# Attention and gated feed-forward on one core: merged steps and new pacing in the second pass, spread vector work elsewhere

## The chip, the cores and the metric

The kernel runs on one core of a Trainium2 chip. The metric is the device time of one execution in microseconds, given as the median of several runs. The core's engines are TensorE (PE in the profile), VectorE (DVE), ScalarE (ACT), GpSimd (POOL) and SyncE (SP, here only the issuer of DMAs). Each executes its own instructions in the order in which the program emits them; semaphores tie the engines together.

## The reference, cut to what matters

Four sequences of 448 tokens with 12 heads of 64 go through causal attention. The result, 1792 rows of 768, is normalised by its root mean square and goes through a gated feed-forward layer with 1536 hidden columns, all in float32.

```python
scores = np.matmul(q, k.transpose(0, 1, 3, 2)) / np.sqrt(64)
scores = np.where(mask, -1e9, scores)            # causal
attn = exp(scores - max) / (sum + 1e-9)
x = np.matmul(attn, v) -> reshaped to (1792, 768)
xn = x / np.sqrt(np.mean(x * x, -1) + 1e-6) * rms_g
g = xn @ w_gate
out = (g * sigmoid(g) * (xn @ w_val)) @ w_out
```

## The kernel before

**Blocks of tokens.** Rows are cut into three blocks: the first 256 queries of two sequences (512 columns), the same of the other two (512), and the rest of all four (768). Attention is cut into 60 units, each with two heads: 12 of kind 0 for block 0, 12 of kind 0 for block 1, and 36 for block 2. Of these 36, each group of six has four of kind 1 (128 queries, 384 keys) and two of kind 2 (64 queries and 448 keys, two sequences at once).

**The steps of a unit.** *Scores* (`steps_s`, L171): matmuls into PSUM (L191), on DVE mask and row minimum (L200), then exp on ACT, a reciprocal on DVE and the division on POOL or ACT, the latter three posted some slots later. *Transposes* (`steps_t`, L233), one step for each head `e`: three or four transposes into a PSUM bank (L248), then one copy to SBUF tile `pt` (L252 on DVE, L254 on ACT). In the second pass all of them use the one bank `t`, so the next step's transposes must wait for the copy. *Products* (`steps_a`, L258): matmuls of `v` and `pt` into bank `a` (L274) and a copy out (L289).

**Slots.** A stretch ahead does the attention of block 0. Then two passes do the feed-forward of block 0 and of block 1, each over 36 weight tiles `s`; one tile is three *slots* (`k0` in 0, 2, 4), and a slot issues six matmuls of 512 columns (L435 to L437, high and low parts of float32 split into two). After its six matmuls a slot may run attention steps: pass 0 those of block 1, pass 1 those of block 2. `AT` (L54) says over how many of the pass's 108 slots the steps are spread, by L851: `while done < goal and (done - at) < (goal - at) * i / AT[w_]`. `tick()` ends a slot, and `post(d, fn)` delays work by `d` slots.

**Steps of the second pass.** `round_of_two` (L750) takes two units p and p+1 in five steps: a *visit* (scores of p+3 and p+4, products of p and p+1), and the transposes of p+2 and of p+3, two steps each. 18 rounds and two steps ahead of them come to 90 steps in pass 1, the last four of them empty, over 77 slots. So 13 slots hold two steps. Two steps, the transposes of unit 25, stand at the end of pass 0; there 37 steps are spread over 101 slots.

**The end of pass 1.** When all steps are done (L871) `x_steps` (L483) scales block 2 (L514), makes the sums of a seven-product scheme for 2x2 blocks (L523) and splits the operands into high and low parts `ch` and `cl` (L473, and L475 on DVE or L102 on POOL), one entry of its list a slot. Besides, DVE makes the low parts `w_l` of every second weight tile (L391) and evicts results `ob` (L443), whose stores to DRAM (L445) stand in SP's one queue with the weight loads. `quad_load` (L560) loads the first weights for block 2 and `quad_prep` (L569) splits them; the fourth one (L564) is posted eight slots after the top of tile 69.

**Block 2 and the end.** Block 2's gate and value products run through `quad_product` and `quad_result` (L582, L596): seven products of nine matmuls for each of 12 weight tiles. Then 21 products of 18 matmuls (L695) make the output. Ahead of them `h_sums` (L674) makes two sums and a difference from the hidden tile for each of three parts, all in the first three products; the difference (L679) is read first by operand 12, which is split beside product 8.

**Root mean square.** `rms` (L330) has one matmul with ones, a square root on ACT and four reciprocals of 128 columns on DVE (L338), one behind the other.

Of the kernel before, what the change touches and what calls it, by code (L numbers as in the profile page):

```python
# [39 lines left out]
ENDS = [max(i for i, u in enumerate(UNITS) if u[0] == g) + 1 for g in range(NG)]  # L40
# [10 lines left out]
WR = 4  # L51
WARM = [9, 0, 0, 2]
EXTRA = 4
AT = [101, 77]  # L54
XT = 768
HX = XT // 2
RING = 6
# [4 lines left out]
def attention_ffn(ctx: ExitStack, tc: tile.TileContext, qk0, qk1, qk2, v, v2, w, g, out, out2):  # L62
# [7 lines left out]
    nc = tc.nc  # L70
# [59 lines left out]
    def post(delay, fn):  # L130
        if delay <= 0:
            fn()
        else:
            later.setdefault(now[0] + delay, []).append(fn)
# [98 lines left out]
    def steps_t(p):  # L233

        if not 0 <= p < len(UNITS):
            return []
        _, kind, _, _, _, _ = UNITS[p]
        pr = hs[p]
        kb = KB[kind]

        def some(e):
            pt = pr["pt", e] = pt_p.tile([P, W], F32, tag=f"pt{e}", name="pt")
            ps = bank("x" if e and p < ENDS[1] + 1 else "t")
            at = 0
            for j in range(NKB[kind]):
                for o, wd in blocks(kind):
                    if kb * j < wd:
                        nc.tensor.transpose(ps[:kb, at: at + P],  # L248
                                            pr["sp"][e][:, o + kb * j: o + kb * (j + 1)], ident)
                        at += P  # L250
            if kind or (e and p < ENDS[0]):
                nc.vector.tensor_copy(pt[:kb, :at], ps[:kb, :at])  # L252
            else:
                nc.scalar.copy(pt[:kb, :at], ps[:kb, :at])  # L254

        return [lambda e=e: some(e) for e in (0, 1)]
# [73 lines left out]
    def rms(b, sq):  # L330

        ps = bank("t")
        nc.tensor.matmul(ps, ones, sq, start=True, stop=True)
        r = rinv[b] = rm_p.tile([P, W], F32, tag="rms", name="rms", bufs=2)
        nc.scalar.activation(r, ps, AF.Sqrt, bias=eps, scale=1.0 / DM)
        for i in range(W // P):
            sl = slice(i * P, (i + 1) * P)
            nc.vector.reciprocal(r[:, sl], r[:, sl])  # L338


    w64 = w.bitcast(I32).rearrange("u p (c t) -> u p c t", t=2)
# [218 lines left out]
    def quad_load(v, n):  # L560
        f, g_ = divmod(v, 2)
        t = wr_p.tile([P, DM], F32, tag="w", name="w_q")
        if n == 3:
            nc.sync.dma_start(out=t[:, : HX], in_=w32[2 * (f + 6) + g_][:, HX:])  # L564
        else:
            nc.sync.dma_start(out=t, in_=(w32[2 * f + g_], wy[v], wz[v])[n])
        wt["q", v, n] = t
# [103 lines left out]
    def h_part(p):  # L671
        return [hid[:, 6 * k: 6 * k + 6, HX * e + P * p: HX * e + P * (p + 1)] for e in (0, 1) for k in (0, 1)]

    def h_sums(p):  # L674
        a11, _, a21, a22 = h_part(p)
        s1, s2 = f2["s", p] = [side["s"].tile([P, 6, P], F32, tag=n, name=n, bufs=3) for n in ("s1", "s2")]
        nc.vector.tensor_tensor(s1, a21, a22, op=ALU.add)  # L677
        nc.vector.tensor_tensor(s2, s1, a11, op=ALU.subtract)  # L678
        nc.vector.tensor_tensor(a21, a11, a21, op=ALU.subtract)  # L679

    def h_operand(q):
# [68 lines left out]
    def round_of_two(p):  # L750


        def visit():
            for q in (p, p + 1):
                post(2, lambda q=q: load_v(q + 2))
            for f in steps_s(p + DP) + steps_s(p + DP + 1):
                f()
            fs = steps_a(p), steps_a(p + 1)
            for i in (0, 1):
                for f in fs:  # L760
                    f[i]()

        return [visit] + [lambda q=q, i=i: (steps_t(q) or 2 * [lambda: None])[i]()
                          for q in (p + 2, p + 3) for i in (0, 1)]


    def warm(n):
# [4 lines left out]
    with tc.manual_schedule():  # L772
# [9 lines left out]
        for p in range(-DP, ENDS[1]):  # L782
            steps += round_steps(p)
            if p + 1 in ENDS:
                ends.append(len(steps))
        steps += [lambda i=i: steps_t(ENDS[1] + 1)[i]() for i in (0, 1)]
        for p in range(ENDS[1], len(UNITS), 2):
            steps += round_of_two(p)
            if p + 2 in ENDS:
                ends.append(len(steps))  # L790
        done = 0
        n_pre = ends[0] + EXTRA
# [11 lines left out]
        n = 0  # L804
# [25 lines left out]
        for s in range(2 * NU):  # L830
            w_ = s // NU
            if s == NU:
                assert len(xh) == 12
                xrs.close()
                side["wrx"] = pool("wrx", 4, ffn1, side="left", reuse_waits="tile")
            if s % NU == 0:
                at, goal = done, ends[w_ + 1] + 2 * (w_ == 0)
            if s + 7 < NU:
                post(T["ld"], lambda s=s: load_w(s + 7))
            n = s + 6 - 2 * NU  # L840
            if n >= 0:
                if n < 4:
                    post(8, lambda n=n: quad_load(0, n))
            elif s + 6 >= NU:
                post(T["ld2" if NU <= s + 6 < NU + 2 * NF else "ld1"], lambda s=s: load_w(s + 6))
            for k0 in (0, 2, 4):
                ks = [k for k in (k0, k0 + 1) if (s, k) not in early]
                if ks:
                    ffn_part(s, ks)
                i = 3 * (s % NU) + k0 // 2 + 1  # L850
                while done < goal and (done - at) < (goal - at) * i / AT[w_]:  # L851
                    steps[done]()
                    done += 1
                if i >= 73 and w_ == 0:
                    split_x()
                if k0 == 0:
                    convert(s + 5)
                if k0 == (0 if s < 3 else 4):
                    split_w(s + 3)
                for fn in prep.pop(now[0], []):  # L860
                    fn()
                if todo:
                    for fn in todo.pop(0):
                        fn()
                n = 3 * (s - 2 * NU + 2) + k0 // 2
                if n in (0, 3, 5):
                    quad_prep(0, (0, 3, 5).index(n))
                if n in (2, 4):
                    quad_load(1, n // 2 - 1)
                tick()  # L870
                if todo is None and done == len(steps) and i >= AT[1] + 1:  # L871
                    assert s % NU >= 2 * NF
                    ffn1.close()
                    att.close()
                    side["xc"] = pool("xc", 1, tail, side="right", reuse_waits="tile")
                    side["sm"] = pool("sm", 1, tail, side="right", reuse_waits="tile")
                    todo = x_steps()
# [49 lines left out]
        for q in range(21):  # L927
            i, p = divmod(q, 3)
            ps_ = out_product(i, p)
            if i:  # L930
                wo_split(3 * (i + 1) + p)
                wo_load(3 * (i + 2) + p)
            out_result(i, p, ps_)
            if not i:
                h_sums(p)
            h_operand(q + 4)


# [46 lines left out]
```

## Time and profile before

| what | value |
|---|---|
| median of 3 runs | 727.82 us (725.52 to 728.54) |
| the profiled execution's own time | 726.79 us |
| its span in the trace | 724.6 us |
| PE busy | 675.3 us, 93% of the span |
| DVE, ACT, POOL busy | 535.8, 370.9, 361.8 us |
| mean granted clock of TensorE | 0.995 |

The span runs from the first to the last instruction of the profiled execution; what lies around it is 2.2 us. PE is busy for most of it, so time can come only from the 49 us in which PE idles, and from stretches in which its clock is granted at less than full speed.

### The profile page before, as it was taken

The page shows a single profiled execution, that of the slowest core. Times are in us where ns is not written, and L with a number is a line of the kernel's source. Part 1 is how long each engine was busy: PE and PEld are TensorE (multiplying, and loading weights), DVE is VectorE, ACT ScalarE, POOL GpSimd, SP SyncE. Part 2 cuts the span into 40 slices and gives each one's busy share as a digit, 9 for nine tenths or more (in the row PEclk, how much of TensorE's full clock was granted, in tenths as well). Part 3 has the DMA queues.
Part 4 walks back from the last instruction along what each step waited for, and adds up shares of the span by engine and source line. Part 5 has one row for each costly group of instructions (what it writes and reads, how often), then busy time and mean ns, then how long its engine had stood idle before and what let it go on. Part 6 is the DMA issues. An engine that isn't in the chain of part 4 may idle for free. (4 is left out here: it accounts for less than half of the span.)

```text
span 724.6 us, 11938 instructions
## 1 busy us (share of the span) xinstructions
PE 675.3 (93%) x4106; PEld 547.4 (76%) x4106; DVE 535.8 (74%) x1029; ACT 370.9 (51%) x832; POOL 361.8 (50%) x313
## 2 busy tenths in 40 slices
PE   9778889999999899989999998999899999999898
PEld 6455567677776666667767676787799999999887
DVE  4976899799998456767676767369386768689773
ACT  6958777777765234346253534335333433355341
POOL 4987445455556334646655565664354536402120
PEclk9999999999999999999999999999999999999999
DMA  7746477867776538575657555422557576452541
GB/s 255 254 146 204 153 261 254 276 223 252 270 237 245 182 113 248 159 249 164 228 169 261 170 181 171 146 99 98 182 176 247 183 250 232 156 154 77 153 119 65
DMA packets 71355, 138.80 MB, mean 192 GB/s; under 512 B 7744, under 2 KB 39232, under 8 KB 71296
## 3 DMA queue, kind: packets, MB, share of 16 engines
q1 hardware_dynamic: 71296, 138.05, 58.1%
q8 instruction: 32, 0.52, 0.3%
q14 instruction: 27, 0.22, 0.1%
HBM read 104.21 MB, written 33.82 MB: 190 GB/s over the span
## 5 line engine op out<-in xcount | busy, mean ns | idle before, releaser
L208 POOL TENSOR_SCALAR sp<-sp,rs 128x384 f32<-128x384 f32 (+3 forms) x132 | 87.1, 677 | 107.3 <-DVE rs L212 106.3
L435 PE MATMUL m_ps<-xh,w_h 128*128 128x512 f32 x282 | 120.2, 426 | 2.5 <-DVE t_sb L459 2.5
L437 PE MATMUL m_ps<-xh,w_l 128*128 128x512 f32 x282 | 111.1, 394 | 1.7 <-POOL w_l L102 1.7
L436 PE MATMUL m_ps<-xl,w_h 128*128 128x512 f32 x282 | 110.5, 392 | 0.0
L203 ACT ACTIVATE sp<-sp,nm 128x384 f32<-128x384 f32 (+3 forms) x168 | 87.2, 522 | 45.6 <-DVE nm L200 45.6
L102 POOL TENSOR_TENSOR a_l<-w_q,a_h 128x768 fp32r<-128x768 f32 x24 | 47.9, 1994 | 69.8 <-ACT a_h L473 69.6
L274 PEld LDWEIGHTS a_ps<-pt,v_r 128*64 128x64 f32 (+1 forms) x864 | 40.4, 137 | 37.6 <-issue 15.1
L274 PE MATMUL a_ps<-pt,v_r 128*64 128x128 f32 (+2 forms) x864 | 57.5, 267 | 10.4 <-DVE pt L252 6.7
L252 DVE COPY pt<-t_ps 128x384 f32<-128x384 f32 (+1 forms) x71 | 42.6, 599 | 32.9 <-PE t_ps L248 32.8
L248 PE MATMUL t_ps<-ident,sp 128*128 128x128 f32 (+1 forms) x309 | 51.4, 278 | 16.6 <-DVE pt L252 11.9
L435 PEld LDWEIGHTS m_ps<-xh,w_h 128*128 128x128 f32 x282 | 53.1, 188 | 14.8 <-issue 4.9
L102 POOL TENSOR_TENSOR w_l<-w_r,w_h 128x768 fp32r<-128x768 f32 x30 | 60.1, 2006 | 8.2 <-ACT w_h L389 8.2
L437 PEld LDWEIGHTS m_ps<-xh,w_l 128*128 128x128 f32 x282 | 52.9, 188 | 14.1 <-POOL w_l L102 2.1
L200 DVE CUSTOM_DVE_ANT_0 sp<-s_ps,mask 128x128 f32<-128x128 f32 (+3 forms) x136 | 49.8, 415 | 18.3 <-PE s_ps L191 16.8
L248 PEld LDWEIGHTS t_ps<-ident,sp 128*128 128x128 f32 (+1 forms) x309 | 36.7, 138 | 34.0 <-POOL sp L208 11.4
L375 POOL TENSOR_SCALAR w<-w 128x768 f32<-128x768 f32 x36 | 43.0, 1193 | 37.1 <-ACT w_c L374 27.9
L436 PEld LDWEIGHTS m_ps<-xl,w_h 128*128 128x128 f32 x282 | 53.3, 189 | 7.5
L435 PE MATMUL m_ps<-hh,w_h 128*128 128x512 f32 x144 | 58.9, 409 | 0.0
L437 PE MATMUL m_ps<-hh,w_l 128*128 128x512 f32 x144 | 57.1, 397 | 1.1 <-POOL w_l L102 0.9
L436 PE MATMUL m_ps<-hl,w_h 128*128 128x512 f32 x144 | 56.8, 394 | 0.0
L102 POOL TENSOR_TENSOR w_l<-w_c,w_h 128x768 fp32r<-128x768 f32 x18 | 38.8, 2157 | 30.0 <-ACT w_h L389 30.0
L377 DVE SCALAR_TENSOR_TENSOR w<-w 128x768 int32<-128x768 int32 x36 | 44.8, 1244 | 10.5 <-POOL w L375 10.4
(176 smaller groups left out, 1704.3 us busy)
## 6 DMA issues: line engine op xcount, KB each, us to landing
w<-in_w SPq DMA_DIRECT2D x36, 768.0 KB, 4.9
w<-w_c SPq DMA_DIRECT2D x36, 384.0 KB, 2.7
w_r<-w SPq DMA_DIRECT2D x36, 384.0 KB, 4.2
qk_r<-in_qk SPq DMA_DIRECT2D x48, 256.0 KB, 4.0
qk_r<-in_qk SPq DMA_DIRECT2D x12, 512.0 KB, 6.0
v_r<-in_v SPq DMA_DIRECT2D x12, 448.0 KB, 4.2
v_r<-in_v SPq DMA_DIRECT2D x24, 192.0 KB, 3.1
wy<-w_r SPq DMA_DIRECT2D x24, 192.0 KB, 5.2
```

Source lines behind the costliest of these rows:

```text
L102: nc.gpsimd.tensor_tensor(out_, a, b, op=op)
L200: nc.vector.tensor_tensor_reduce(out=sp, in0=ps, in1=mk, scale=nsc, scalar=3.0e38, op0=ALU.add, op1=ALU.min, accum_out=nm)
L203: post(T["exp" if p >= ENDS[0] else "exp0"], lambda: nc.scalar.activation(sp, sp, AF.Exp, bias=nm, scale=-1.0, accum_out=sm))
L208: pr["norms"].append(lambda: nc.gpsimd.tensor_scalar(sp, sp, rs, 1.0, op0=ALU.mult, op1=ALU.mult))
L248: nc.tensor.transpose(ps[:kb, at: at + P], pr["sp"][e][:, o + kb * j: o + kb * (j + 1)], ident)
L252: nc.vector.tensor_copy(pt[:kb, :at], ps[:kb, :at])
L274: nc.tensor.matmul(av_ps[e * D: (e + 1) * D, p % 2, q0: q0 + n], raw_v[p][:kb, h, j, e, :], pr["pt", e][:kb, a0: a0 + n], start=(j == 0), ...
L375: (T["c1"], lambda: nc.gpsimd.tensor_scalar(hf_, hf_, 0.0, 1.0, op0=ALU.mult, op1=ALU.mult)),
L377: (T["c2" if s >= 5 else "c20"], lambda: nc.vector.scalar_tensor_tensor(out=lo, in0=lo, scalar=29, in1=hi, op0=ALU.logical_shift_right, op ...
L435: nc.tensor.matmul(ps, wh[:, k, :], mh, start=(first and k == ks[0]), stop=False)
L436: nc.tensor.matmul(ps, wh[:, k, :], ml, start=False, stop=False)
L437: nc.tensor.matmul(ps, wl[:, k, :], mh, start=False, stop=(last and k == 5))
```

## The change

- `AT` goes from [101, 77] to [108, 73]: the steps of pass 0 are spread over all 108 slots, those of pass 1 over 73.
- `round_of_two` has four steps a round instead of five. The second transposes of unit p+1 move out of the round before into the first step, ahead of the scores and products, on PE and on DVE.
- The second transposes of unit 25 go from pass 0 into pass 1. The three steps behind the last visit, which would be empty, are deleted. Pass 0 now has 36 steps in 108 slots (one in every third slot), pass 1 has 69 in 73 slots (never two in one). The last visit comes in slot 72 instead of 73, and `x_steps` begins in slot 75 instead of 79.
- For block 1 the four reciprocals of `rms` are posted one a slot.
- The fourth weight load of block 2 is posted four slots after the top of tile 69 instead of eight, so it stands ahead of the third one, and of the store of the result of slot 102, in SP's queue.
- The difference in `h_sums` becomes `h_difference`, called beside products 6 to 8 instead of 0 to 2.

```diff
-AT = [101, 77]
+AT = [108, 73]
...
         for i in range(W // P):
             sl = slice(i * P, (i + 1) * P)
-            nc.vector.reciprocal(r[:, sl], r[:, sl])
+            post(i if b else 0, lambda sl=sl: nc.vector.reciprocal(r[:, sl], r[:, sl]))
...
         nc.vector.tensor_tensor(s2, s1, a11, op=ALU.subtract)
+
+    def h_difference(p):
+        a11, _, a21, _ = h_part(p)
         nc.vector.tensor_tensor(a21, a11, a21, op=ALU.subtract)
...
-        return [visit] + [lambda q=q, i=i: (steps_t(q) or 2 * [lambda: None])[i]()
-                          for q in (p + 2, p + 3) for i in (0, 1)]
+        def transposes(q, i):
+            fs = steps_t(q)
+            if fs:
+                fs[i]()
+
+        def last():
+            transposes(p + 1, 1)
+            visit()
+
+        return [last] + [lambda q=q, i=i: transposes(q, i) for q, i in ((p + 2, 0), (p + 2, 1), (p + 3, 0))]
...
-        steps += [lambda i=i: steps_t(ENDS[1] + 1)[i]() for i in (0, 1)]
+        steps.append(lambda: steps_t(ENDS[1] + 1)[0]())
         for p in range(ENDS[1], len(UNITS), 2):
             steps += round_of_two(p)
             if p + 2 in ENDS:
+                del steps[-3:]
                 ends.append(len(steps))
...
-                at, goal = done, ends[w_ + 1] + 2 * (w_ == 0)
+                at, goal = done, ends[w_ + 1] + (w_ == 0)
...
-                    post(8, lambda n=n: quad_load(0, n))
+                    post(8 if n < 3 else 4, lambda n=n: quad_load(0, n))
...
-            if not i:
+            if i == 0:
                 h_sums(p)
+            elif i == 2:
+                h_difference(p)
             h_operand(q + 4)
```

## Rows read from the trace of the kernel before

**Rows 1.** Busy time of each engine in the two passes (stretch, length, engines, granted clock).

```profile
71.45:256.42 184.97, 173.86 (x848) 131.55 (x847) 159.89 (x237) 123.19 (x263) 95.02 (x62) 0.99 0.67 231
256.42:464.28 207.86, 195.54 (x1543) 143.24 (x1542) 142.41 (x356) 90.80 (x227) 118.62 (x111) 1.00 0.60 192
```

**Rows 2.** PE's waits in 256.42 to 464.28 us: total, times, longest.

```profile
PE t_ps L248 <- DVE pt L252: 8.9, 8, 1.8
PE t_ps L248 <- POOL sp L208: 3.3, 4, 1.2
```

**Rows 3.** Single slots of pass 1, or ten bare ones, by stretch; columns as in Rows 1.

```profile
483.35:496.95 13.60, 13.60 (x62) 11.26 (x60) 12.06 (x20) 6.31 (x13) 7.73 (x8) 1.00 0.31 107
286.37:288.08 1.71, 1.71 (x12) 1.40 (x11) 0.69 (x3) 1.07 (x2) 0.70 (x2) 1.00 0.87 288
288.08:291.34 3.26, 2.25 (x16) 1.73 (x14) 2.29 (x4) 0.62 (x1) 3.26 (x4) 1.00 0.55 191
291.34:296.12 4.78, 4.78 (x45) 2.82 (x43) 2.69 (x9) 1.52 (x6) 3.42 (x3) 1.00 0.02 4
336.96:342.07 5.11, 5.11 (x48) 3.22 (x46) 4.54 (x12) 2.58 (x6) 3.21 (x3) 1.00 0.41 142
418.64:424.15 5.51, 5.51 (x86) 4.15 (x83) 4.45 (x12) 2.44 (x7) 4.36 (x4) 1.00 0.25 91
```

**Rows 4.** Timeline inside the last of these slots (start, duration, engine, line).

```profile
420.92 0.68 DVE L252 COPY pt<-t_ps 112x512 f32<-112x512 f32 x1
...
422.13 2.08 PE L274 MATMUL a_ps<-pt,v_r 112*64 112x64 f32 x64
```

**Rows 5.** The end of pass 0: one stretch of three slots, then DVE and PE in it.

```profile
237.69:246.87 9.18, 6.25 (x22) 4.79 (x21) 5.72 (x8) 1.56 (x2) 4.35 (x2) 0.81 0.56 195
...
235.84 3.37 DVE L338 RECIPROCAL rms<-rms 128x128 f32<-128x128 f32 x4
...
242.14 0.71 PE L248 MATMUL t_ps<-ident,sp 128*128 128x128 f32 x3 [2.93 <-DVE pt L252]
```

**Rows 6.** The last slots of pass 1: busy time, L514 alone, then DVE and PE.

```profile
476.74:505.19 28.45, 28.22 (x124) 22.87 (x123) 26.91 (x41) 13.81 (x27) 16.45 (x12) 1.00 0.36 119
...
477.34:481.55 4.21, 4.21 (x8) 1.00 0.71 249
...
476.74 0.69 DVE L443 SCALAR_TENSOR_TENSOR ob<-m_ps,rms 128x512 f32<-128x512 f32 x1 [6.19 <-PE m_ps L437]
...
495.97 1.77 DVE L391 TENSOR_TENSOR w_l<-w_r,w_h 128x768 fp32r<-128x768 f32 x1
...
497.79 0.50 PE L437 MATMUL m_ps<-hh,w_l 128*128 128x512 f32 x1 [0.23 <-DVE w_l L391]
```

**Rows 7.** The start of block 2's products: timeline of ACT, DVE and PE.

```profile
513.69 0.51 ACT L473 CAST a_h<-w_q 128x384 fp32r<-128x384 f32 x1 [6.30 <-DMA w_q<-w]
...
518.30 0.55 DVE L606 TENSOR_TENSOR u<-m,s_ps 128x384 f32<-128x384 f32 x1 [3.50 <-DMA out_t<-ob]
...
514.64 0.44 PE L578 MATMUL m_ps<-ch,a_h 128*128 128x384 f32 x1 [1.35 <-ACT m L601]
...
522.96 0.44 PE L578 MATMUL y_ps<-ch,a_h 128*128 128x384 f32 x1 [1.81 <-DVE c L612]
```

**Rows 8.** The output products: products 3 and 4, product 6, product 7; then DVE and PE.

```profile
657.72:663.96 6.24, 6.24 (x37) 6.24 (x37) 6.21 (x7) 4.01 (x6) 2.00 (x1) 1.00 0.11 37
667.08:674.28 7.20, 4.72 (x19) 3.77 (x19) 6.26 (x6) 2.16 (x5) 2.21 (x1) 0.87 0.61 185
674.28:678.14 3.86, 3.86 (x19) 3.86 (x19) 2.39 (x3) 1.54 (x2) 0.00 (x0) 0.79 0.62 170
...
656.82 0.95 DVE L679 TENSOR_TENSOR hid<-hid 128x768 f32<-128x768 f32 x1
...
669.01 2.59 DVE L475 TENSOR_TENSOR ol<-s,oh 128x768 fp32r<-128x768 f32 x1
...
672.52 0.69 PE L578 MATMUL s_ps<-a_l,oh 128*128 128x384 f32 x1 [2.06 <-DVE a_l L475]
```

## The prediction

> **What bounds the kernel now.** I read the busy time by stage first. PE is busy 195.5 of 207.9 us in the attention part of pass 1 and 173.9 of 185.0 us in pass 0, and no other engine comes near that in pass 1 (DVE 142.4); in pass 0 DVE is next with 159.9 [rows 1]. So PE's queue sets the time, and an edit gains only what it takes from PE's idle time or from a stretch at a lower clock. Next I read who PE waits for in pass 1: transposes, and nothing else. Eight waits are for the copy that empties bank t (8.9 us), four for the division on POOL (3.3 us) [rows 2]. Then I cut pass 1 into slots at the first matmul of each, and compared slots of the same content. At last I read the places outside this stretch with a PE gap over 1 us that the change touches: the end of pass 0 [rows 5], the start of block 2 [rows 7], output product 6 [rows 8]. Two gaps of over 2 us do more than idle: behind them the mean granted clock of the stretch is 0.81 and 0.79, that is, PE runs for a while at the lower of its two levels, 1.2 GHz [rows 5, 8].
>
> **Part 1, four steps a round in pass 1.** A bare slot costs 13.60 / 10 = 1.36 us, a slot with one transposes step 1.71, so it costs 0.35; two transposes steps in one slot should cost 2.06, but the slot shown took 3.26, 1.20 more, of which PE idles 3.26 - 2.25 = 1.01 [rows 3]. Eight such slots make the 8.9 us of waits. The four waits on POOL come where only two slots lie between a visit and the transposes that need its softmax; with three slots there is none. In the new order pass 1 has 69 steps in 73 slots. No slot has two steps, so no transposes stand straight behind others, and the first transposes of unit p+3 come at least three slots behind their scores. Both kinds of wait lose their cause: 8.9 + 3.3 = 12.2 us, and by the slot shown each of the 12 costs another 1.20 - 1.01 = 0.19 in refilling PE, 2.3 together: 14.5 us. The matmuls themselves stay the same in number.
>
> What is added is that each of the rounds has its transposes of p+1 right ahead of the scores, so products of p+1 wait for a copy that was issued in the same slot. The trace of before has this very slot twice, by the accident of its pacing. One took 5.11 us, where a visit of the same kind alone took 4.78 and the step adds 0.35: 5.13 expected, so the merger was free. The other, with the wider units, took 5.51, all of it PE busy [rows 3]. There the copy ran from 420.92 to 421.60, and the products began at 422.13, behind four pairs of score matmuls [rows 4]. The scores are the cover, about half a microsecond over what was needed, and the products of p come ahead of those of p+1 besides. If that cover is gone, each of the 17 mergers costs up to 1.20, the price of the uncovered slot, 20 us in all; the other bound is 0. I take 2.0, nearer to the two slots that show it free, for those rounds in which DVE is late. DVE's own work stays the same while the stretch shortens: 142.4 / (207.9 - 12.5) is 73% instead of 69%, no bound. **Gain 12.5 (14.5 less 2.0).**
>
> **Part 2, the end of pass 0.** Three slots there took 9.18 us where three bare ones and one step make 3 x 1.36 + 0.35 = 4.43 [rows 3, 5]. The excess of 4.75 has one cause: the four reciprocals hold DVE for 3.37 us, the copy out of bank t stands behind them, the next transposes wait 2.93 us, and the clock falls [rows 5]. In the new order the two steps of unit 25 are three slots apart (106 and the first of pass 1) and the reciprocals come one a slot, at the end of slots 103 to 106, where weight conversion, which filled DVE, is over. They are first read by the eviction behind slot 3 of pass 1, five slots later, so the delay costs nothing. The first waits for the square root on ACT; behind it on DVE are only a copy and evictions that come later. **Gain 4.5**, with bounds 3 (a gap of about 1 us stays) and 4.75. The rest of pass 0 only gets its steps further apart, 9 slots a round instead of 8.2. I give it nothing: DVE's 86% there [rows 1] eases a little, but every step now falls in the slot behind an eviction.
>
> **Part 3, the last 36 slots.** `x_steps` begins four slots sooner against the matmuls. On DVE this moves a long chain ahead of a deadline. Before, DVE was busy 26.9 of the 28.45 us from the eviction at 476.74 to 505.19: 12 scalings, 12 sums, 12 low parts, two `w_l` and two evictions. The `w_l` that slot 100 needs stood only behind three of the low parts, ended at 497.74, and still held PE for 0.23 us [rows 6]. Now it stands behind all twelve. Six scalings are done before that first `ob`, so ahead of it there remain 28.45 less 3.2 (six scalings at 4.21 / 8), 1.8 (the `w_l` itself), 0.7 (an eviction) and 1.4 (most of its idle 1.54): 21.4 us, start 498.1 in the times of before, end 499.1 with 0.95 for itself or 499.9 with 1.77. Against 497.74 that is 1.4 to 2.2 us more. The low parts can also be quicker, since POOL then has less beside them; bounds 0 and 2.6. **Loss 1.4.** The columns step now comes three slots (4.1 us) behind the last visit instead of six; I take no new wait for it.
>
> **Part 4, the start of block 2.** ACT waited 6.30 us for the fourth weights; the copy of the first product stands behind that split, and PE waited 1.35 for it. DVE then waited 3.50 for the store of the last result, which stood in SP's queue behind the same weights' buffer; this became PE's 1.81 us [rows 7]. SP's queue was late altogether because the store of slot 96 waited for its eviction at the end of the long chain. Now that eviction comes right behind the `w_l` of slot 100, and the fourth load is issued two places sooner: it has some seven slots (9 us) to land. The buffer that it takes moves the others by one place; the last load now waits for the third weights' split instead, on POOL, done about when the last slot ends, so the last store behind it need not cost DVE its 3.50. **Gain 3.0 of 1.35 + 1.81**; bounds 0 and 4.
>
> **Part 5, the sums.** Products 3 and 4 took 3.12 us each. Products 6 and 7 took 7.20 + 3.86, 4.82 over that [rows 8]: PE waited for `a_l` behind three differences of 0.95, then ran on at the low clock. Without them DVE comes to the low parts 2.8 us sooner, and the operand split that took 2.59 instead of 0.95, beside a POOL split, then falls ahead of that [rows 8]. Product 6 would find all three `a_l`. The differences now lie beside products 6 to 8. There DVE has about 3.1 us of work a product (a low part, an eviction, an operand, a difference) against PE's 3.12: full, so I leave 0.8 for a new wait. **Gain 4.0**, bounds 1.5 and 4.8.
> The Trainium skill, page "SBUF — State Buffer", section "SBUF: two separate sides", says that a VectorE operation with two SBUF inputs and a GpSimd operation shut each other out for a whole instruction, and speaks so against this move. The 2.59 us row agrees; each difference that meets a POOL split would take about 1.6 more by it, and one of them beside product 6 would leave 2.4 of these 4.0.
>
> **Sum.** 12.5 + 4.5 - 1.4 + 3.0 + 4.0 = 22.6 us from the profiled execution's own 726.79: 704.2. That execution lies 1.0 below the median of the runs (727.82), so I forecast 705.2.
>
> **Rivals.**
> *The chain on DVE takes the place of the old waits.* If the low parts meet POOL throughout, `w_l` ends 2.6 later than before and PE idles over 2 us; the clock then falls as behind product 6, where 4.82 were lost for 2.48 of idling (7.20 - 4.72) [rows 8]; I add 1.5. The stores then also come late and Part 4 gives nothing: 705.2 + (4.1 - 1.4) + 3.0 = 710.9. For it: DVE's chain has no free time. Against it: 1.77 for a `w_l` is already one beside POOL [rows 6], and 0.23 of waiting was all that it cost.
> *Pass 0 suffers from its even pacing.* If the steps, all behind evictions now, wait about 1.0 in each of eleven rounds, as PE's 1.01 in the slot with two steps [rows 3]: 716. Against it: a step in most slots of before cost nothing.
> *The merger isn't covered.* Most of the 17 wait for the copy, and the gain of pass 1 is lost, the waits having only moved: 705.2 + 18 = 723, no measurable change.
> *Slower.* In the merged slots the copy stands on DVE behind other work of the second pass (sums of weights, `w_l`), comes over 2 us late in most rounds, and each gap also lowers the clock; at 4 us a round (product 6 and 7 lost 4.8 so) six rounds eat all that is gained, and eight end at 705 + 32 = 737. It decides if the copy comes later than the scores and the products of p last. Both merged slots speak against it.
>
> **How the numbers follow.** The forecast (699 to 709) has 0.55, the chain 0.20, pass 0 0.10, no cover 0.10, slower 0.05. The range takes the first two and half of the third: 699 (no residue in Parts 1, 3 and 5) to 715. About 0.5%, 3.6 us, is what a measurement of this kernel can tell from no change. Faster by more than that: 0.55 + 0.20 + 0.10 + 0.05 (half of "no cover") = 0.90; within it 0.05; slower 0.05.
>
> **What the profile of the changed kernel would show.** Part 1: PE's waits of transposes for the copy and for POOL gone, a merged slot at 5.1 to 5.5 us; wrong, if products (L274) wait for the copy (L252). Part 2: no 2.9 us gap and clock 1.00 at the end of pass 0. Part 3: a wait of PE at L437 for `w_l` in slot 100 of 1.5 to 2 us. Part 4: no wait of L578 for ACT's m or DVE's c at the start. Part 5: product 6 at 3.1 to 4 us. The prediction fails if waits of the same sum appear elsewhere on PE.

## Result and profile after

The changed kernel takes 700.07 us, the median of 4 runs (698.40 to 702.16), against 727.39 (725.52 to 728.54) for the kernel before: a ratio of 0.9628, 95% interval 0.9594 to 0.9663. The forecast was 705.2 with a range of 699 to 715. The profiled execution of the changed kernel took 702.16, the longest of its four, so the difference of the two profiled spans, 724.6 - 700.4 = 24.2 us, is less than the 27.3 us between the medians. By the medians the time lies 5.1 us under the forecast and 1.1 above the lower end of the range. The parts below are summed to the 24.2.

The table cuts both executions at the same places of the program: the first matmul of slot 3, of slot 1 of pass 1, of slot 74 of pass 1, of block 2, and of the first output product.

| stage (us) | before | after | difference | predicted |
|---|---|---|---|---|
| ahead of slot 3 | 71.45 | 71.16 | -0.3 | 0 |
| pass 0 (Part 2) | 184.97 | 177.28 | -7.7 | -4.5 |
| pass 1, slots 1 to 73 (Part 1) | 202.28 | 189.92 | -12.4 | -12.5 |
| pass 1, slots 74 to 108 (Part 3) | 51.28 | 57.36 | +6.1 | +1.4 |
| block 2's products (Part 4) | 137.85 | 132.62 | -5.2 | -3.0 |
| output products (Part 5) | 76.77 | 72.06 | -4.7 | -4.0 |
| span | 724.6 | 700.4 | -24.2 | -22.6 |

The sum of this profile came out within 2 us because two errors met: the gains of Parts 2, 4 and 5 were put 6.1 too small in all, the loss of Part 3 4.7 too small. That they cancel is luck. The stages after, from the view by stretch (stretch, length, busy PE, PEld, DVE, ACT, POOL with instructions, granted clock, DMA share, GB/s):

```profile
71.16:248.44 177.28, 171.72 (x843) 131.63 (x842) 158.56 (x236) 123.84 (x263) 96.56 (x62) 0.98 0.70 241
248.44:438.36 189.92, 189.16 (x1523) 141.39 (x1522) 143.69 (x356) 89.88 (x226) 114.94 (x109) 1.00 0.65 205
438.36:495.72 57.36, 53.48 (x228) 43.37 (x227) 33.64 (x48) 21.24 (x39) 26.51 (x21) 0.94 0.37 121
495.72:628.34 132.62, 131.79 (x757) 130.88 (x756) 96.62 (x140) 54.37 (x90) 56.45 (x28) 1.00 0.62 203
628.34:700.40 72.06, 66.52 (x379) 65.30 (x378) 55.53 (x63) 29.70 (x42) 12.13 (x6) 1.00 0.37 110
```

In slots 1 to 73 PE is now busy 189.16 of 189.92 us: nothing is left to take there but work. The one stretch that grew, slots 74 to 108, has PE idle for 3.9 us and a mean clock of 0.94.

The waits of PE in slots 1 to 73 (total, times, longest), in place of [rows 2], and two merged slots of the kinds in [rows 3]:

```profile
PE a_ps L274 <- DVE pt L252: 0.7, 2, 0.5
...
323.35:328.47 5.12, 5.12 (x49) 3.23 (x47) 4.53 (x12) 2.59 (x6) 3.20 (x3) 1.00 0.48 124
400.57:406.07 5.50, 5.50 (x85) 4.15 (x82) 4.43 (x12) 2.48 (x7) 4.36 (x4) 1.00 0.33 122
```

The twelve waits of transposes, 12.2 us, are gone. Both merged slots cost what the two accidental ones of before cost (5.11 and 5.51), with PE busy throughout. Only two products waited for the copy, 0.7 us together.

Slots 100, and 101 with 102, then DVE's and PE's timeline there (start, duration, engine, line, in brackets the idle time before it and what ended it). The row that answers in [rows 6] is PE's wait of 0.23:

```profile
476.54:482.91 6.37, 2.49 (x8) 1.68 (x6) 5.91 (x8) 0.83 (x1) 2.14 (x1) 0.78 0.07 27
482.91:487.54 4.63, 4.63 (x14) 3.64 (x13) 0.00 (x0) 0.00 (x0) 0.00 (x0) 0.56 0.73 231
...
468.19 7.50 DVE L475 TENSOR_TENSOR cl<-t,ch 128x384 fp32r<-128x384 f32 x6
475.62 1.48 DVE L475 TENSOR_TENSOR cl<-xq,ch 128x384 fp32r<-128x384 f32 x3
477.02 3.09 DVE L475 TENSOR_TENSOR cl<-t,ch 128x384 fp32r<-128x384 f32 x3
480.04 0.94 DVE L391 TENSOR_TENSOR w_l<-w_r,w_h 128x768 fp32r<-128x768 f32 x1
...
481.04 0.79 PE L437 MATMUL m_ps<-hh,w_l 128*128 128x512 f32 x1 [3.88 <-DVE w_l L391]
```

The four DVE rows follow one another without a gap: twelve low parts from 468.19 to 480.04, then the `w_l` that slot 100 waits for. PE stands for 3.88 us and then runs at a mean clock of 0.56, near the lower of its two levels (1.2 of 2.4 GHz). Slots 100 to 102 take 6.37 + 4.63 = 11.00 us where three bare ones take 4.08 [rows 3].

The start of block 2, in place of [rows 7]:

```profile
495.69 0.52 ACT L473 CAST a_h<-w_q 128x384 fp32r<-128x384 f32 x1 [3.20 <-PE m_ps L436]
497.50 0.48 ACT L601 COPY m<-m_ps 128x384 f32<-128x384 f32 x1 [1.30 <-PE m_ps L578]
500.59 0.55 DVE L606 TENSOR_TENSOR u<-m,s_ps 128x384 f32<-128x384 f32 x1 [3.51 <-PE m_ps L578]
```

ACT's split no longer waits for the weights but for a buffer that PE frees, and ACT's copy and DVE's sum wait for PE's products: the two engines wait for PE, not PE for them. Neither of PE's waits (1.35 and 1.81) is left.

### The profile page after: what moved, and what is told of

Same layout as the page of the kernel before. It is cut to its first block, busy times and chain, and to the rows that moved or that the text cites. A ratio compares the mean times of both kernels' runs of the same rounds, so it can differ in the third digit from the quotient of the medians.

```text
span 700.4 us, 11930 instructions
## 1 busy us (share of the span) xinstructions
PE 671.0 (96%) x4106; PEld 550.9 (79%) x4106; DVE 536.9 (77%) x1029; ACT 371.6 (53%) x832; POOL 361.9 (52%) x313
## 5 line engine op out<-in xcount | busy, mean ns | idle before, releaser
L208 POOL TENSOR_SCALAR sp<-sp,rs 128x384 f32<-128x384 f32 (+3 forms) x132 | 89.5, 696 | 95.8 <-DVE rs L212 84.8
L375 POOL TENSOR_SCALAR w<-w 128x768 f32<-128x768 f32 x36 | 46.5, 1292 | 53.1 <-ACT w_c L374 47.0
L473 ACT CAST a_h<-w_q 128x768 fp32r<-128x768 f32 (+1 forms) x48 | 35.0, 753 | 24.9 <-PE m_ps L436 19.1
```

The lines of the kernel that those rows point to most:

```text
L208: pr["norms"].append(lambda: nc.gpsimd.tensor_scalar(sp, sp, rs, 1.0, op0=ALU.mult, op1=ALU.mult))
L375: (T["c1"], lambda: nc.gpsimd.tensor_scalar(hf_, hf_, 0.0, 1.0, op0=ALU.mult, op1=ALU.mult)),
```

## Experiments

All kernels compute the whole of the reference. "Before" in a ratio is the kernel before, run on the same chip.

**Part 1 alone, on the kernel before.** The second pass's order, its pacing (73 slots) and the old start of `x_steps`; nothing else.

```diff
-AT = [101, 77]
+AT = [101, 73]
...
+        def last():
+            if p > ENDS[1]:
+                transposes(p + 1, 1)
+            visit()
...
-                if todo is None and done == len(steps) and i >= AT[1] + 1:
+                if todo is None and done == len(steps) and i >= 78:
```

> The kernel before with Part 1 alone: four steps a round, no empty steps, over 73 slots; pass 0, the reciprocals, the start of block 2's preparation (slot 79), the loads and the sums stay as before. By Part 1 slots 1 to 73 of pass 1 fall from 202.3 to 189.5, by 12.5 to 13, the other stages stay within 1.5 us of before (pass 0 185, slots 74 to 108 51.3, output 76.8), and the time is 12 to 13 below the kernel before. Rival (the gain needs the other edits, or is given back later, in slots 74 to 108 or block 2): less than 10.

Measured: 711.87 us (709.76 and 713.99), ratio 0.9806, 0.9766 to 0.9846, 13.6 us under the 725.5 of before. Slots 1 to 73:

```profile
254.02:443.34 189.32, 188.74 (x1519) 140.98 (x1518) 142.77 (x355) 89.91 (x226) 115.13 (x109) 1.00 0.63 205
```

That is 13.0 less than before; every other stage stayed within 1.5 us. So the gain of this stage belongs to Part 1 and needs nothing of the other parts.

**Part 1 without its cover.** The second transposes of p+1 go behind the scores, right ahead of the products.

```diff
             for f in steps_s(p + DP) + steps_s(p + DP + 1):
                 f()
+            transposes(p + 1, 1)
...
         def last():
-            transposes(p + 1, 1)
             visit()
```

> The changed kernel with the order in the merged slot turned: scores first, then the transposes of p+1, then the products. Theory (the scores on PE are the cover for the copy): the copy now has only the products of p, some 0.8 us, in front, and on DVE it stands behind four row minima of about 0.5 each; products wait 1 to 2 us in each of 17 rounds, and where the wait nears 2 the clock falls: slots 1 to 73 of pass 1 take 210 to 235 us instead of 189.7. Rival (one transposes step in a slot is what counts, the place in the slot doesn't): 190 to 193.

Measured: 717.88 us (717.16 to 719.85), ratio 0.9915, 0.9882 to 0.9949. Its stretch of slots 1 to 73, PE's waits in it, then PE and DVE in one merged slot:

```profile
247.50:453.23 205.73, 196.92 (x1522) 142.92 (x1521) 140.98 (x356) 90.02 (x226) 114.97 (x109) 1.00 0.57 189
...
PE a_ps L274 <- DVE pt L252: 8.8, 17, 1.6
...
284.85 0.55 PE L248 MATMUL t_ps<-ident,sp 128*128 128x128 f32 x3
285.32 1.09 PE L274 MATMUL a_ps<-pt,v_r 128*64 128x128 f32 x14
286.80 0.87 PE L274 MATMUL a_ps<-pt,v_r 128*64 128x128 f32 x10 [0.39 <-DVE pt L252]
...
285.65 0.62 DVE L200 CUSTOM_DVE_ANT_0 sp<-y_ps,mask 128x448 f32<-128x448 f32 x1
...
286.19 0.55 DVE L252 COPY pt<-t_ps 128x384 f32<-128x384 f32 x1
```

One wait in each of the 17 mergers that have scores, fourteen of 0.27 to 0.39 us and three of 1.00 to 1.63, and a stretch 15.8 us longer than after: 0.93 a merger, within the bounds of 0 and 1.20. It is less than the 210 to 235 us that were expected, and the clock did not fall. All of the gain is gone with the order inside the slot alone, while the spacing of the steps stays.

This edit changes two things at once: the scores no longer stand between transposes and products on PE, and on DVE the copy now stands behind the row minima of those scores. The rows speak for the second. The transposes end at 285.40, but the copy starts at 286.19, behind the last row minimum. Started 0.25 after the transposes, it would have ended by about 286.2 (an estimate from these rows), before the products of p end at 286.41, and there would be no wait. In all 17 rounds the copy comes right behind the last row minimum, 0.69 to 2.05 us after the transposes. Besides, the last merger of the changed kernel, in slot 72, has no scores and no wait. So what makes the merger free is that the transposes, and with them the copy, come ahead of the scores; that the scores are needed as a cover on PE is not shown.

**The changed kernel once more**, without an edit, to tell what varies from run to run.

> The changed kernel once more, unedited, beside the others, to see how far its stages repeat: slots 1 to 73 of pass 1 at 189.7, slots 74 to 108 at 56 to 57.4, block 2 at 132.6 to 134, output stage at 72 to 73.6, pass 0 at 174.8 to 177.3; ratio to the kernel before 0.963. If the wait in slot 100 is a matter of chance and not of order, slots 74 to 108 come out under 54 here.

Measured: 702.78 us (700.14 to 705.32), ratio 0.9669, 0.9644 to 0.9693. Slots 74 to 108 took 57.48 us with a wait of 3.92 for `w_l`: the loss of Part 3 is no accident. (The five other runs that keep that order on DVE show it too: waits of 3.88 to 3.92, 56.2 to 57.2 us.) Block 2 took 134.0 us and the output products 73.6, each 1.4 to 1.5 more than in the first profile, and pass 0 178.1. Differences of such a size between two stretches are not read as effects below.

**Part 3 undone:** `x_steps` begins where it did before.

```diff
-                if todo is None and done == len(steps) and i >= AT[1] + 1:
+                if todo is None and done == len(steps) and i >= 78:
```

> The changed kernel, but the operand preparation for block 2 begins in slot 79 again (from slot 78 on) instead of slot 75. The changed kernel's time is 700.07; in its trace the slots 74 to 108 of pass 1 took 57.4 us against 51.3 before, because PE waited 3.88 us for a w_l in slot 100 and then ran three slots at the lower clock. Theory (the early start puts all twelve low parts ahead of that w_l on DVE): the wait goes back to about 0.2, slots 74 to 108 take 51 to 52, and at most 2 us come back at the start of block 2: 694 to 696. Rival (the wait has to do with the faster pass, weights arriving later or DVE further behind in general): the wait stays over 2 us, 698 to 700.

Measured: 698.0 us (695.82 to 699.17), ratio 0.9626, 0.9590 to 0.9662. Slots 74 to 108 and block 2:

```profile
435.22:486.45 51.23, 50.92 (x227) 41.28 (x226) 32.63 (x48) 20.97 (x39) 27.00 (x21) 1.00 0.39 126
486.45:622.04 135.59, 132.89 (x757) 130.82 (x756) 96.88 (x140) 54.34 (x90) 57.89 (x29) 1.00 0.61 201
```

The wait in slot 100 is 0.31 us and the clock 1.00: the 6.1 us are back. But block 2 is 3.0 us longer than in the first profile of the changed kernel and 1.6 longer than when it ran again: PE waits there 1.09 and 0.43 us for DVE's `c` in the first 25 us, where the one has no such wait and the other one of 0.28. So the early start is what costs in slot 100, and by the wait of 1.09 it also pays in block 2, though 1.6 us is hardly more than what varies from run to run. The time missed the expected 694 to 696, and its ratio is that of the changed kernel (0.9628): over whole runs the early start is not shown to cost or to pay.

**The `w_l` of slot 100 taken off DVE:** POOL makes it.

```diff
-            if s % 2 == 0 and s < NU or s > NU + 2 * NF and s % 2:
+            if s % 2 == 0 and s < NU or s > NU + 2 * NF and s % 2 and s != 69:
```

> The changed kernel with one edit: the low part of weight tile 69 is made on POOL instead of DVE. If the wait in slot 100 is only this one instruction's place in DVE's queue, PE's wait of 3.88 and the low clock behind it go, slots 74 to 108 take about 50.5 instead of 57.4, and the time is 693 to 694. Rival: POOL and DVE shut each other out, the next w_l on DVE or POOL (tiles 70 and 71) comes late instead, and 2 us or more of the wait stay: 696 to 699.

Measured: 698.0 us (693.63 to 699.57), ratio 0.9617, 0.9563 to 0.9670; slots 74 to 108 took 54.07. DVE's low parts, the eviction behind them, and PE:

```profile
465.87 9.15 DVE L475 TENSOR_TENSOR cl<-t,ch 128x384 fp32r<-128x384 f32 x6
...
479.40 0.68 DVE L443 SCALAR_TENSOR_TENSOR ob<-m_ps,rms 128x512 f32<-128x512 f32 x1
...
480.23 0.47 PE L435 MATMUL m_ps<-hh,w_h 128*128 128x512 f32 x1 [1.82 <-DVE ob L443]
```

PE no longer waits for `w_l`, but three slots later for the eviction that frees its bank and that stands behind the same low parts. Half of the loss is back, and the time lies in the rival's range (696 to 699). And the first six low parts took 9.15 us instead of 7.50, with one more subtraction on POOL beside them. The cause is the length of the whole chain, not the one `w_l`.

**The chain stretched:** empty slots ahead of the last two operand groups, so that the early start stays but `w_l` and the evictions come between the low parts.

```diff
         for i, x in ((1, op(2, 2)), (3, op(5, 2)), (4, []), (6, [])):
+            todo += [[] for _ in range({4: 3, 6: 1}.get(i, 0))]
             todo.append(op(i, 0) + op(i, 1) + op(i, 2) + x)
```

> The changed kernel with the last two operand groups of block 2's preparation put off by three and four entries, so that on DVE the w_l of slot 100 stands behind six low parts instead of twelve, and the eviction of slot 96 behind nine. Theory (only the order on DVE's queue makes the wait): no wait over 0.3 us in slots 97 to 108, these slots of pass 1 (74 to 108) take 50.3 to 51 instead of 56 to 57, block 2 stays at 132.6 to 133, and the time is 6 to 7 us below that of the changed kernel, a ratio of 0.953 to the kernel before. Rival (DVE has no room there at all): the wait moves to the eviction in slot 103 or to block 2's start as with POOL, and 3 us or less are gained, ratio 0.958 or more.

Measured: 693.46 us (692.18 to 695.45), ratio 0.9571, 0.9521 to 0.9622. Slots 74 to 108, block 2, and DVE:

```profile
436.57:486.95 50.38, 50.38 (x227) 41.46 (x226) 32.99 (x48) 21.32 (x39) 26.74 (x21) 1.00 0.42 136
486.95:621.63 134.68, 132.28 (x757) 130.85 (x756) 95.43 (x140) 54.43 (x90) 56.37 (x28) 1.00 0.61 200
...
466.40 7.49 DVE L475 TENSOR_TENSOR cl<-t,ch 128x384 fp32r<-128x384 f32 x6
473.81 0.95 DVE L391 TENSOR_TENSOR w_l<-w_r,w_h 128x768 fp32r<-128x768 f32 x1
```

The same six low parts take the same 7.49 us, but `w_l` comes right behind them. PE is busy 50.38 of 50.38 us, 7.0 less than after and 0.9 less than before. Its four runs lie below all eight of the changed kernel (698.40 to 705.32). Block 2 missed the expected 132.6 to 133: PE waits there 0.51 and 1.10 for DVE's `c`, 21 and 55 us behind its start.

**The fourth load in its old place**, first in the changed kernel, then with the stretched chain.

```diff
-                    post(8 if n < 3 else 4, lambda n=n: quad_load(0, n))
+                    post(8, lambda n=n: quad_load(0, n))
```

> The changed kernel with the fourth weight load of block 2 posted eight slots late again. Part 4 has two causes in one: the load's place in SP's queue, and the earlier end of the chain on DVE. If the load's place counts, ACT waits for it again, PE waits 1 us or more for ACT's m or DVE's c at the start, and block 2 takes 135.5 to 137 instead of 132.6 to 133. If it was the store behind the late chain, block 2 stays at 132.6 to 133.5.

> The version with the late operand groups, and the fourth load eight slots late again. With the wait in slot 100 in place, the load's place cost nothing (block 2 at 133.5), but that wait and the low clock behind it also gave the load some 7 us more to land. Here the wait is gone. If the load's place counts on its own, ACT waits for it again, PE waits about 1 us for ACT's m, and block 2 takes 136 or more instead of 134.7. If only the end of the chain on DVE counted, no such wait appears and block 2 stays within 1 us of 134.7.

Measured: 701.05 us (700.90 and 701.21), ratio 0.9657, 0.9636 to 0.9678, for the first; 694.1 us (692.3 to 694.85), ratio 0.9598, 0.9538 to 0.9659, for the second. Block 2, and ACT's copy of the first product, in the second:

```profile
485.12:618.46 133.34, 132.09 (x757) 130.89 (x756) 95.62 (x140) 54.44 (x90) 56.09 (x28) 1.00 0.62 202
...
486.90 0.48 ACT L602 COPY m<-m_ps 128x384 f32<-128x384 f32 x1 [1.29 <-PE m_ps L579]
```

With the load back in its old place the copy waits for PE as it does after (by 1.29 and 1.30), and PE does not wait for it at the start. Block 2 stays at 133.3 to 133.5, inside the 132.6 to 134.0 of the two profiles of the changed kernel. Where the chain on DVE is early, the place of the load is worth nothing that can be seen. Where it is late, the wait for the copy is 1.35 in the kernel before, 0.89 and 0.37 in two kernels with the same code there (the spread reciprocals below, and Part 1 alone), and none with the late chain but the early load: there the place may count for that much.

**The reciprocals in a row again**, the steps of unit 25 staying apart:

```diff
-            post(i if b else 0, lambda sl=sl: nc.vector.reciprocal(r[:, sl], r[:, sl]))
+            nc.vector.reciprocal(r[:, sl], r[:, sl])
```

> The changed kernel with the four reciprocals of block 1 in a row again. Theory of the prediction's Part 2 (the block of four on DVE is the one cause of the gap at the end of pass 0): the gap of about 2.9 and the low clock return, 4.75 us: 704 to 705. Rival (what mattered is that the two transposes steps of unit 25 no longer stand three slots apart behind that block: the first is now two slots behind the square root, the second in the next pass): less than 1 us, 699.5 to 701.

Measured: 699.13 us (698.67 to 700.83), ratio 0.9649, 0.9616 to 0.9683. Pass 0, and DVE at its end:

```profile
69.98:244.80 174.82, 171.03 (x844) 131.71 (x842) 159.26 (x236) 123.81 (x263) 96.51 (x62) 0.98 0.71 244
...
238.52 3.39 DVE L338 RECIPROCAL rms<-rms 128x128 f32<-128x128 f32 x4 [1.02 <-ACT rms L335]
242.24 0.56 DVE L252 COPY pt<-t_ps 128x384 f32<-128x384 f32 x1 [0.34 <-PE t_ps L248]
```

The block of 3.39 us is back and costs nothing: it ends before PE has written the transposes whose copy would stand behind it (the copy waits 0.34 for PE).

**The reciprocals spread, on the kernel before**, with its two steps still side by side: the line above the other way round.

> The kernel before with the one edit that block 1's reciprocals come one a slot. In the changed kernel a block of four in a row cost nothing. By Part 2 of the prediction (the block on DVE is the one cause of the 2.93 us gap) three slots at the end of pass 0 fall from 9.2 to 4.5 or 5, pass 0 from 185.0 to about 180.5. If the cause is that unit 25's two steps stand right behind the square root while DVE is still full of weight conversion, the reciprocals meet the same copy two at a time, the gap stays at 1 to 2.9 us, and pass 0 takes 182 to 185.

Measured: 721.04 us (716.69 to 724.00), ratio 0.9945, 0.9913 to 0.9976. Pass 0 and PE's gap at its end, in place of the 2.93 of [rows 5]:

```profile
70.51:251.64 181.13, 173.43 (x847) 131.39 (x846) 160.52 (x237) 123.54 (x263) 95.67 (x62) 0.99 0.69 236
...
238.95 0.44 PE L248 MATMUL t_ps<-ident,sp 128*128 128x128 f32 x2 [1.30 <-DVE pt L252]
```

1.30 is left, what two transposes side by side cost anyway (1.01 in [rows 3]). Pass 0 is 3.8 us shorter than before (2.9 against the kernel with Part 1 alone, which has the pass 0 of before). The gap of 2.93 needed both: a block on DVE, and two steps side by side with their copy behind it. Spreading the reciprocals alone removes more than half of it, and in the changed kernel, with the steps apart, the block leaves none.

**Pass 0 with the old pacing**, the rest as in the changed kernel:

```diff
-AT = [108, 73]
+AT = [101, 73]
```

> The changed kernel with the steps of pass 0 over 101 slots again instead of 108 (36 steps, so 8.4 slots a round instead of 9). Pass 0 took 185.0 us before and 174.8 to 177.3 with the change, of which the prediction put 4.5 down to the gap at its end and nothing to the pacing. If the even pacing is what gave the rest (some 3 to 5 us), pass 0 takes 178 to 181 here, with waits of PE for DVE, ACT or POOL spread over it as before. If the pacing gives nothing, pass 0 stays at 175 to 177.

Measured: 704.11 us (703.86 and 704.36), ratio 0.9724, 0.9659 to 0.9790. Pass 0 took 177.19 us, with PE busy for 171.80. That lies inside the 174.1 to 178.1 that pass 0 took in the kernels of this study that share its code with the changed one. That the slower pacing gains anything is not shown; two runs can't tell it.

**The sums together again:**

```diff
             if i == 0:
                 h_sums(p)
-            elif i == 2:
                 h_difference(p)
```

> The changed kernel with the three differences back beside output products 0 to 2. Theory of Part 5: the output stage takes 4.7 us more (72.1 to about 76.8), products 6 and 7 at 7.2 and 3.9 instead of 3.1, time 704.8. Rival: the gain there came with the earlier stages (weights loaded sooner), and the stage stays within 1 us of 72.1: 700 to 701.

Measured: 703.53 us (701.64 to 704.16), ratio 0.9701, 0.9667 to 0.9736. The output products:

```profile
624.76:701.70 76.94, 68.94 (x379) 66.76 (x378) 56.32 (x63) 29.83 (x42) 12.17 (x6) 0.98 0.35 103
```

4.9 us longer than after; PE's waits for `a_l` of 0.40 and 2.06 are back and so is the lower mean clock. Part 5 does what it was said to do.

## Why the prediction was right, point by point

The time and the places of the gains came as forecast. The sizes were less sure than they look: three of the five parts fell outside the bounds that the prediction gave them (Part 2: 7.7, bounds 3 and 4.75; Part 3: 6.1, bounds 0 and 2.6; Part 4: 5.2, bounds 0 and 4).

**Part 1 was right in cause and size.** 12.5 predicted, 12.4 measured, 13.0 by itself. The step that carried it, reading the price of the merger from two slots of before that had it by accident, was repeated by the slots after to 0.01 us, and putting the transposes behind the scores cost 15.8 us. Two smaller terms were off and cancelled. The residue of 2.0 for a late DVE came as 0.7 of waits. The 2.3 for refilling PE came as 0.8: in slots 1 to 73 PE was busy for 189.96 us before and 189.16 after. And the reason given, the scores as a cover for the copy, is not the one that the rows of the kernel without it show: by the estimate made there, the products of p, which the prediction named besides, would have been cover enough.

**Part 2 was right in place, too small in size, and wrong in its cause as put.** "The excess has one cause", the block of reciprocals, fell: with the block back nothing is lost, and with the block alone removed 1.30 of the gap stays. The cause is the block together with the two steps side by side. The size, 7.7 against 4.5, is more than the end of the pass held. PE's waits of pass 0, before and after (total, times, longest):

```profile
PE t_ps L248 <- DVE pt L252: 2.9, 1, 2.9
...
PE m_ps L437 <- POOL w_l L102: 2.6, 2, 1.7
PE m_ps L435 <- DVE t_sb L459: 2.5, 2, 1.4
```

```profile
PE m_ps L435 <- DVE rs L212: 3.7, 3, 2.1
...
PE m_ps L437 <- POOL w_l L102: 0.4, 1, 0.4
```

Besides the gap of 2.9, the waits for POOL's `w_l` and DVE's `t_sb`, 5.1 us together, went but for 0.4, and waits for `rs` of 3.7 came (2.0 in the profile with the sums together, where pass 0 is the same code). In the nine profiles with this code pass 0 took 174.1 to 178.1 us, against 185.0 and 184.0 in the two with that of before. "I give it nothing" was the step that failed: moving the steps of the first pass to other slots removed waits that the prediction had not read. Of the pacing the record shows this: with 101 slots a wait for `t_sb` of 2.7 is there and none for `rs`, with 108 it is the other way round in all nine, so the pacing exchanged one for the other. The `w_l` wait is small with the old pacing too (0.7); which of the moves took it away stays open.

**Part 3 was right in mechanism, mis-sized in one term.** The chain ahead of `w_l` was put at 21.4 us from the first `ob`; that eviction began at 456.26, so `w_l` should have started at 477.6. It started at 480.04, 2.4 later. The term that failed is the twelve low parts. The 21.4 took them over at their length in the kernel before:

```profile
493.73 2.31 DVE L475 TENSOR_TENSOR cl<-t,ch 128x384 fp32r<-128x384 f32 x3
...
497.66 3.14 DVE L475 TENSOR_TENSOR cl<-t,ch 128x384 fp32r<-128x384 f32 x3
...
501.33 2.54 DVE L475 TENSOR_TENSOR cl<-xq,ch 128x384 fp32r<-128x384 f32 x3
503.79 1.48 DVE L475 TENSOR_TENSOR cl<-t,ch 128x384 fp32r<-128x384 f32 x3
```

That is 9.47 us; after, 7.50 + 1.48 + 3.09 = 12.07, 2.6 more. (The sums ahead of them took 0.4 less.) The first six took 1.25 each, beside two low parts (1.02 and 1.13) and two `w_l` (2.16 and 1.89) on POOL; the three at 1.48 took 0.49 each, with POOL idle, before as after. "The low parts can also be quicker, since POOL then has less beside them" was the wrong way round: nine of the twelve met POOL, as before, and it had five operations of 8.34 us in all beside the twelve instead of four of 7.39. The Trainium skill's page "SBUF — State Buffer", section "SBUF: two separate sides", has the rule that bears on it (a VectorE operation with two SBUF inputs and a GpSimd operation shut each other out); these rows agree, 7.50 growing to 9.15 with one more POOL operation. The prediction weighed that rule in Part 5, where it came to nothing, and not here, where these operations are of the same kind.

The wait follows from it: 0.23 + 1.4 + 2.4 = 4.0 against 3.88, where 1.5 to 2 had been named as the sign. The rest of the loss, 11.00 - 4.08 - 3.88 = 3.0 us, is the lower clock behind the gap (1.9 to 3.2 in the seven profiles that have the gap), which the forecast had not priced, as no gap of this length was in it. The rival of the DVE chain had priced it, at 4.1 in all, less than the 6.1 that came; its first half happened.

**Part 4 was right in size on the average of the runs, but not in its causes.** The rival's second half, that the stores then come late and Part 4 gives nothing, did not happen: behind the last `w_l` the evictions had time, and block 2 is 5.2 us shorter. Over the profiles that share their code in block 2 it took 135.4 to 137.9 us before (three) and 132.6 to 134.0 after (six), 3.3 less on the average, against 3.0 predicted. The load's new place, which the prediction counted as half of the reason, shows nothing when put back.

The other half was the store: DVE's wait of 3.50 for it was said to become PE's 1.81 [rows 7]. The stretched chain speaks against that. First DVE and POOL before, behind that wait, then DVE in the kernel with the stretched chain:

```profile
518.77 2.55 DVE L475 TENSOR_TENSOR a_l<-w_q,a_h 128x768 fp32r<-128x768 f32 x1
...
518.66 1.85 POOL L102 TENSOR_TENSOR a_l<-w_q,a_h 128x768 fp32r<-128x768 f32 x1 [1.42 <-ACT a_h L473]
```

```profile
491.61 0.55 DVE L607 TENSOR_TENSOR u<-m,s_ps 128x384 f32<-128x384 f32 x1 [3.30 <-DMA out_t<-ob]
492.08 0.95 DVE L475 TENSOR_TENSOR a_l<-w_q,a_h 128x768 fp32r<-128x768 f32 x1
```

There DVE waits 3.30 for the store, nearly as long, and PE has no wait at the start of block 2. What differs is the low part behind it: 0.95 us instead of the 2.55 that it took when a POOL split had begun 0.11 ahead of it. It took 2.53 in Part 1 alone and 2.07 with Part 3 undone, with waits of PE of 1.78 and 1.09 behind it, and 0.95 in the changed kernel. So some 1.6 of the 1.81 are that meeting, by an estimate from these rows. Undoing Part 3 brings it back, and block 2 is 1.6 to 3.0 longer; how far the meeting hangs on the late store, and where the rest of the gain comes from, stays open.

**Part 5 was right.** 4.7 against 4.0, 4.9 when undone. Products 6 and 7 now take 6.24 together instead of 7.20 + 3.86 [rows 8]. Their stretch, and one of the three differences on DVE:

```profile
647.65:653.89 6.24, 6.24 (x38) 6.24 (x37) 5.34 (x6) 3.53 (x5) 1.85 (x1) 1.00 0.79 234
...
658.34 2.31 DVE L682 TENSOR_TENSOR hid<-hid 128x768 f32<-128x768 f32 x1
```

This one met a POOL split and took 2.31 instead of 0.94, 1.4 more, near the 1.6 that the prediction took from the 2.59 us row; the other two took 0.94. PE did not wait for it, so the 0.8 left for a new wait was not needed.

## What to carry over

A small operation with a deadline is priced by the whole queue of its engine ahead of it, and the batch in that queue by the rows that show it beside the engines it will meet, not by what is left over in another stretch. Two pieces of work that wait for each other's buffer can share a slot at no cost if independent matmuls stand between them and the copy does not stand behind a batch of other work on its engine; look for the slot in which the trace already shows it. And when a move pays in one stage and costs in the next, stretch the moved chain around the operation with the deadline instead of undoing the move: that kept most of both here (693.5 us).

## What the runs showed of the hardware

The same small gaps did not always lower TensorE's clock. In the output products PE has two waits close to each other, of 0.96 and 0.68 us in the profile of the changed kernel and of 0.96 and 0.69 when it ran again. For some 3.5 us behind them the granted clock was 1.00 in the first and 0.54 in the second, with nearly the same busy time on the other engines:

```profile
680.40:684.00 3.60, 3.60 (x23) 3.60 (x22) 3.60 (x5) 1.57 (x2) 1.30 (x1) 1.00 0.19 67
```

```profile
682.00:685.50 3.50, 3.50 (x13) 3.50 (x12) 3.50 (x5) 1.56 (x2) 1.25 (x1) 0.54 0.18 65
```

All 14 profiles have this pair of waits; the clock behind it was 0.54 to 0.60 in four and 1.00 in ten. With the differences moved, the stage took 73.6 us in those four and 72.0 to 72.1 in the six others, which is some of the spread between runs of one kernel. Single waits in the kernel without cover, fourteen of 0.27 to 0.39 us and three of 1.00 to 1.63, never lowered it. One wait of 1.82 did (0.58 in the 3.8 us behind it, with the `w_l` on POOL), and the wait of 3.9 did in all seven profiles that have it (0.68 to 0.83 over slots 100 to 102). What decides in between stays open.
